# Inverting 32x32 triangles on one Trainium2 core: by columns on VectorE, or as 16x16 blocks with small matmuls for the block below

## The chip, the core and the metric

The kernel runs on one core of a Trainium2 chip. A core has TensorE (PE, matrix products into PSUM), VectorE (DVE), ScalarE (ACT), GpSimd (POOL) and a queue engine (SP) that starts transfers. Each works through its own list of instructions in order; semaphores hold an instruction until what it needs is there. The metric is the device time of one execution in microseconds. All data are float32.

## The reference

The reference has two stages. The first is a linear recurrence over 768 time steps for 4 batches and 8 heads, with a 40x40 state for each of these 32 pairs:

```
y[:, :, t] = np.einsum('bhd,bhde->bhe', rt, state)
Sa = np.einsum('bhde,bhe->bhd', state, at)
state_decay = state * wt[:, :, None, :] - np.einsum('bhd,bhe->bhde', Sa, bt)
state = state_decay + np.einsum('bhd,bhe->bhde', vt, kt)
```

The second takes the outputs as 3072 rows of 320 values. Rows with a positive skip score go to the best of 8 experts (a two-layer network with a ReLU, 320 to 1024 to 320); its result, times a gate, is added to the row. Other rows pass unchanged.

## The kernel before

**Chunks.** The recurrence is worked in 24 chunks of 32 time steps (`for c in range(NC)` in `attn`, lines 469 to 576). Inside a chunk the steps depend on each other through a strictly triangular 32x32 matrix for each of the 32 (batch, head) pairs. Its unit-triangular inverse turns the chunk into matrix products. Four chunks make a phase (`ph, j = divmod(c, 4)`). One "h" is the material of two chunks, so a phase uses two of them, and the 128 triangles of a phase (32 pairs, four chunks) are inverted together, one triangle to a partition.

**What a chunk does**, for each half `x` of the heads (16 pairs): `rs` multiplies the queries with the state; `ux` (line 299) forms the right-hand sides, 128x288 values in PSUM that ACT copies to `UXs`; `uq` (line 310) multiplies them with the inverses in `TB`, and four ACT copies (line 317) put the result into `R1`; POOL masks it (line 319); `sst` (line 320) forms the next state, `yy` (line 342) the output. The next chunk's `rs` needs this chunk's `sst`. The two halves are interleaved by hand. In `uq`, a matrix of `TB` is 128x128, with four 32x32 inverses on its diagonal and zeros elsewhere, and four matmuls of 128 rows, 128 columns and a moving width of 72 do one half.

**Making the inverses.** `m1` (line 154) forms the triangles by small matmuls, for the phase after, and ACT puts them into `AB`. `tinv(ph)` (line 210) inverts them on DVE:

- line 213 transposes `AB` in 32x32 blocks, so that a partition holds one triangle;
- lines 216 and 217 mask, 218 and 219 set the diagonal; columns 0 to 7 of the inverse lie in PSUM (`X0`, tile `px`), columns 8 to 31 in SBUF (`Xi`, in the pool `M`);
- lines 221 to 231 are the solve: 30 steps, each an outer product of a column of the triangle with a row of the inverse (line 228) and a subtraction (line 230), the two groups of columns interleaved;
- line 232 lets ACT copy `X0` beside the rest, and four transposes of 32 partitions by 1024 elements (line 237) put the inverses on the diagonal blocks of `TB`.

`tinv` is a generator. The chunk loop calls `T()` 11 times per chunk (between the pieces above), and each call emits one step; in chunks 1 and 3 every second call emits two. For phases after the first it starts with the last two calls of a phase's first chunk (line 556; in chunk 1 at line 505), and what is left at the end of the phase's fourth chunk is emitted there (line 576). Five phases have one: it works during chunks 1 to 3, 4 to 7, 8 to 11, 12 to 15 and 16 to 19. In the last phase there is none.

**The first phase** is inverted in setup by `tinv0` (line 239), which already uses blocks: the two 16x16 triangles on the diagonal of a 32x32 one are solved together (line 254 the product, 256 the subtraction, 14 steps), and the block below them comes from two sets of small matmuls (`s1`, line 269; `s2`, line 279). `full` (line 271) copies the diagonal blocks to `TB` in four copies of 32 partitions.

**Order.** The order on PE, ACT and DVE is the order of the program (`manual_schedule`); POOL's too in setup. The scans (lines 114 and 126, 1040 elements along a partition) stand in the chunks with even number. DVE also multiplies `rs`'s result by the decay in those chunks (line 296), which `ux` waits for.

Of the kernel before, what the change touches and what calls it, by code (L numbers as in the profile page):

```python
# [57 lines left out]
def attn(ctx,tc,i,m,out,X):  # L58
# [3 lines left out]
    cp=P("const",1); wk=P("wk",1); wk2=P("wk2",2); wk3=P("wk3",3); wk4=P("wk4",4)  # L62
# [91 lines left out]
    def m1(h,x,c,ev=None,late=None,FE=None):  # L154
        if h>=NH: return
        n=h%NL; KB=H[h]['KB']
        if h%2==0 and x==0 and c==0: AB[0]=sq(AB_) if h else sq(a_)
        ab=AB[0]
        p=ps_p.tile([128,4,2,32],F32)
        for hh in range(4):  # L160
            for bb in range(4):
                u=bb*4+hh
                TE.matmul(p[32*bb:32*bb+32,hh],L1[x][n][:,u,c,:],KB[:,u,c],start=True,stop=True)
        o=x*16+(h%2)*8+c
        A.copy(ab[:,:,o:o+7:2].rearrange("p s u -> p u s"),p[:,:,1,:])
        if c==0: an[0]+=1
        if c==0: AT[0]=AT_[an[0]%2].rearrange("p (h c t) -> p h c t",h=4,c=2) if h!=1 else TBa[2][:,8+2*x:10+2*x].rearrange("p h (a t) -> p (h a t)",t=32).rearrange("p (h c t) -> p h c t",h=4,c=2)
        at=AT[0]
        def fin():
            (FE or G).tensor_tensor(at.rearrange("p h c s -> p (h c) s"),at.rearrange("p h c s -> p (h c) s"),mQ.unsqueeze(1).broadcast_to([128,8,32]),ALU.mult)  # L170
            for bb in range(4):
                SP.dma_start(L1[x][n][ao[x]:ao[x]+32,bb*4:bb*4+4].rearrange("p u c t -> p (u c t)"),at[32*bb:32*bb+32].rearrange("p h c s -> p (h c s)"))
        def evac():
            V.transpose(at[:,:,c],p[:,:,0,:])
            if c==1 and late is not None: late.append(fin)
            elif c==1: fin()
        if ev is None: evac()
        else: ev.append(evac)
# [31 lines left out]
    def tinv(ph):  # L210
        ab=AB[0]
        NLt=sq(NL_)
        V.transpose(NLt.rearrange("p a b -> p (a b)"),ab.rearrange("p a b -> p (a b)"))
        Xi=sq(X_)
        X0=ps_x.tile([128,32,SPL],F32)
        V.tensor_tensor(X0,NLt[:,0:SPL].rearrange("p s t -> p t s"),m.mT[:,:,0:SPL],ALU.mult)
        V.tensor_tensor(Xi[:,:,SPL:32],NLt[:,SPL:32].rearrange("p s t -> p t s"),m.mT[:,:,SPL:32],ALU.mult)
        V.memset(X0.rearrange("p a b -> p (a b)")[:,0:SPL*SPL:SPL+1],-1.0)
        V.memset(Xi.rearrange("p a b -> p (a b)")[:,33*SPL::33],-1.0)
        yield  # L220
        for i in range(1,31):
            q=[]
            for g,(j,lo,hi,X) in enumerate(((i,0,min(i,SPL),X0),(i+SPL,SPL,i+SPL,Xi))):
                if j>30: continue
                n=31-j; k=hi-lo
                tmp=tmp_[g]
                tv=tmp[:,:n*k].rearrange("p (a b) -> p a b",b=k)
                V.tensor_tensor(tv,NLt[:,j,j+1:32].unsqueeze(2).broadcast_to([128,n,k]),X[:,j,lo:hi].unsqueeze(1).broadcast_to([128,n,k]),ALU.mult)  # L228
                q.append((tv,X[:,j+1:32,lo:hi]))
            for tv,xv in q: V.tensor_tensor(xv,xv,tv,ALU.subtract)  # L230
            yield
        A.copy(Xi[:,:,0:SPL],X0)  # L232
        s0=(2*ph)%NTB; s1=(2*ph+1)%NTB
        for b in range(4):
            q=slice(32*b,32*b+32)
            t0=TBa[s0]; d=bass.AP(t0.tensor,t0[q].offset,(tuple(t0[q].ap[0]),(TBa[s1].offset-t0.offset,2),(128,16),(1,128)))
            V.transpose(d.rearrange("p h (x f) m -> p m x h f",x=2)[:,q],Xi[q])  # L237
            yield
    def tinv0(Xi):
# [9 lines left out]
        for j in range(1,15):  # L249
# [7 lines left out]
            yield  # L257
        DB=TBa[2][:,12:16].rearrange("p h m -> p (h m)").rearrange("p (a b) -> p a b",a=16)
        V.transpose(fa(NLt[:,16:32]),fa(Xi[:,16:32]))
# [4 lines left out]
        def s1(w,c):  # L264
# [5 lines left out]
            Z[w,c]=wk2.tile([128,8,16],F32,tag="Z",name="Z"); A.copy(Z[w,c],p)  # L270
        def full(w,E):
            for b in range(4):
                q=slice(32*b,32*b+32)
                (V.tensor_copy,A.copy)[E[b]](TBa[w][q,:,q].rearrange("p (x f) m -> p x f m",x=2),NLt[q].rearrange("p m (x h f) -> p h x f m",x=2,h=2)[:,w])
# [35 lines left out]
    def uq(c,x):  # L310
# [3 lines left out]
        for hh in range(4):  # L314
            TE.matmul(UQ[:,hh,:],Tb[:,x*8+hh*2+c%2,:],UXd[x][:,hh,:],start=True,stop=True)  # L315
        for b in range(4):
# [45 lines left out]
    if 1:  # L362

        with tc.manual_schedule(engines={ET.Pool}):
# [104 lines left out]
        for c in range(NC):  # L469
# [144 lines left out]
class Moe:  # L614
    def __init__(s,ctx,tc,i,out,cp):
# [293 lines left out]
```

## Time and profile before

| | us |
|---|---|
| median of 3 runs (689.51 to 695.32) | 689.55 |
| the profiled execution | 686.84 |
| its span | 685.0 |
| setup, to chunk 1's `ux` | 82.9 |
| chunks 1 to 23 and the rows' last routing, to about | 520 |
| the experts, from there to the end | 165 |

The span is the time from the first to the last instruction that the profiler shows. In rows of groups, an entry reads: line, engine, operation, what is written `<-` what is read, the shapes, `x` the count, then the busy time in us and the mean time of one in ns, then the idle time of the engine just before them and what ended it. A matmul in float32 appears as two records, each with a weight load (PEld). [...]

### The profile page before, as it was taken

How to read it: one execution, taken by the hardware profiler on the slowest of the kernel's cores; microseconds unless marked ns; L12 is line 12 of the kernel's file. 1: busy time of each engine (PE TensorE's matmuls, PEld its weight loads, DVE VectorE, ACT ScalarE, POOL GpSimd, SP SyncE). 2: the span in 40 equal slices, each digit the busy share in tenths (PEclk: the TensorE clock that was granted, in tenths of full speed). 3: DMA queues.
4: the chain of work that ended last, by engine and by line, in shares of the span. 5: the costliest groups of instructions: out<-in, count | busy, mean ns of one | idle time of the engine just before them, and what ended most of it. 6: DMA issues, size and time to landing. Idle time of an engine off the chain costs nothing.

```text
span 685.0 us, 31223 instructions
## 1 busy us (share of the span) xinstructions
PE 553.0 (81%) x13620; PEld 473.5 (69%) x13620; DVE 516.1 (75%) x1201; ACT 422.7 (62%) x1154; POOL 324.2 (47%) x248
## 2 busy tenths in 40 slices
PE   5678586778776789866898678997978799999995
PEld 2445475667665668655787567776767689999995
DVE  7999678876997779977699774785339366889881
ACT  6545564576864758747687475877686454444540
POOL 5483942736546365463554533131322236666661
PEclk9788878578996777969779687798897999999998
DMA  7672755352443514435244242435256347677210
GB/s 185 185 239 98 194 138 180 109 161 58 125 132 102 163 50 121 141 102 166 60 129 131 73 126 71 104 110 185 73 158 170 108 127 221 215 214 226 87 49 23
DMA packets 67437, 90.91 MB, mean 133 GB/s; under 512 B 32564, under 2 KB 54657, under 8 KB 65806
## 3 DMA queue, kind: packets, MB, share of 16 engines
q1 hardware_dynamic: 62350, 74.05, 37.2%
q0 software_dynamic: 4944, 14.80, 6.8%
q8 instruction: 109, 1.79, 1.1%
q14 instruction: 34, 0.28, 0.1%
HBM read 74.03 MB, written 17.08 MB: 133 GB/s over the span
## 4 chain that ended last, share of the span: by engine, by line
PE 37%; DVE 29%; ACT 11%; issue 10%; DMA 4%; POOL 3%; POOLq 0%; DVEq 0%; ACTq 0%
DVE M L228 5%; PE pc L786 4%; PE pc L315 4%; PE ps L797 4%; DVE M L126 4%; DVE TB L237 4%; ACT R1t L317 3%; PE ps L327 3%; PE pc L306 3%; PE px L786 2%; PE pc L292 2%; DVE M L230 2%; PE py L797 2%; PE ps L332 2%; ACT L2t L188 2%
## 5 line engine op out<-in xcount | busy, mean ns | idle before, releaser
L319 POOL TENSOR_TENSOR R1t<-R1t,mc 64x512 f32<-64x512 f32 x46 | 62.2, 1353 | 152.2 <-ACT R1t L317 123.7
L317 ACT COPY R1t<-pc 32x288 f32<-32x288 f32 x192 | 74.8, 389 | 30.6 <-PE pc L315 27.5
L315 PE MATMUL pc<-UXs,TB 128*128 128x72 f32 x384 | 66.4, 328 | 0.1
L143 POOL TENSOR_TENSOR WR<-WR,M 128x1024 f32<-128x1024 f32 (+1 forms) x19 | 52.0, 2748 | 23.0 <-DVE M L114 16.9
L734 POOL TENSOR_TENSOR WL<-WR,WH 128x1280 fp32r<-128x1280 f32 (+1 forms) x21 | 57.6, 2779 | 8.7 <-ACT WH L733 8.6
L327 PE MATMUL ps<-R1t,L2t 128*40 128x40 f32 x1472 | 52.4, 228 | 10.9 <-ACT R1t L317 5.1
L315 PEld LDWEIGHTS pc<-UXs,TB 128*128 128x128 f32 x384 | 58.8, 234 | 3.4 <-issue 1.0
L188 ACT COPY L2t<-pq 64x160 f32<-64x160 f32 x184 | 52.6, 286 | 7.0 <-PE pq L185 4.7
L327 PEld LDWEIGHTS ps<-R1t,L2t 128*40 128x40 f32 x1472 | 42.7, 139 | 20.3 <-ACT R1t L317 11.7
L209 ACT COPY R1t<-pq 32x128 f32<-32x128 f32 x184 | 47.0, 256 | 6.5 <-issue 3.0
L228 DVE TENSOR_TENSOR M<-M 128x22 f32<-128x22 f32 (+10 forms) x110 | 49.7, 452 | 0.0
L237 DVE STREAM_TRANSPOSE TB<-M 32x1024 f32<-32x1024 f32 x20 | 38.4, 1919 | 13.7 <-ACT M L232 13.5
L292 PE MATMUL pc<-rvt,SS 128*40 128x32 f32 x1472 | 44.9, 218 | 3.7 <-issue 3.6
L340 ACT COPY SS<-ps 40x320 f32<-40x320 f32 x92 | 38.6, 419 | 14.5 <-PE ps L332 13.0
L688 POOL DMA_INDIRECT xg<-XS,ix x24 | 25.0, 1040 | 46.5 <-DMA xg<-XS,ix 20.9
L292 PEld LDWEIGHTS pc<-rvt,SS 128*40 128x40 f32 x1472 | 38.6, 137 | 11.7 <-issue 8.7
L332 PE MATMUL ps<-L2t,R1t 128*40 128x40 f32 x1472 | 42.7, 220 | 0.4 <-issue 0.4
L308 ACT COPY UXs<-pc 128x288 f32<-128x288 f32 x48 | 19.2, 400 | 36.1 <-PE pc L306 32.1
L230 DVE TENSOR_TENSOR px<-px,M 128x168 f32<-128x168 f32 (+8 forms) x150 | 39.1, 261 | 1.4
L733 ACT CAST WH<-WR 128x1024 fp32r<-128x1024 f32 (+1 forms) x35 | 39.6, 1132 | 0.0
L332 PEld LDWEIGHTS ps<-L2t,R1t 128*40 128x40 f32 x1472 | 38.8, 136 | 0.5 <-issue 0.5
L228 DVE TENSOR_TENSOR M<-M,px 128x168 f32<-128x168 f32 (+8 forms) x150 | 37.0, 247 | 1.7
(244 smaller groups left out, 1577.5 us busy)
## 6 DMA issues: line engine op xcount, KB each, us to landing
rvt<-rv POOLq DMA_DIRECT2D x21, 512.0 KB, 4.6
WR<-kb SPq DMA_DIRECT2D x10, 1024.0 KB
WR<-w SPq DMA_DIRECT2D x16, 640.0 KB
WR<-w SPq DMA_DIRECT2D x16, 512.0 KB
M<-wt SPq DMA_DIRECT2D x9, 520.5 KB
M<-at SPq DMA_DIRECT2D x8, 512.0 KB
WR<-w SPq DMA_DIRECT2D x16, 256.0 KB
R1t<-vt SPq DMA_DIRECT2D x48, 80.0 KB
```

Of the source, the lines that this page charges most:

```text
L143: E.tensor_tensor(H[h]['KB'][0:NR(h),:,:,q,:],H[h]['KB'][0:NR(h),:,:,q,:],v4(Wi)[0:NR(h)],ALU.mult)
L188: A.copy(L2[x][h%NL2][64-64*x:128-64*x,c,bb*4:bb*4+4,:],pt[64*c:64*c+64,:,64*x:64*x+40])
L228: V.tensor_tensor(tv,NLt[:,j,j+1:32].unsqueeze(2).broadcast_to([128,n,k]),X[:,j,lo:hi].unsqueeze(1).broadcast_to([128,n,k]),ALU.mult)
L230: for tv,xv in q: V.tensor_tensor(xv,xv,tv,ALU.subtract)
L237: V.transpose(d.rearrange("p h (x f) m -> p m x h f",x=2)[:,q],Xi[q])
L292: TE.matmul(RS[s,v,:],SS[x][:,b//2,v,:],rr[:,b%2,2*hh+x,:],start=True,stop=True)
L315: TE.matmul(UQ[:,hh,:],Tb[:,x*8+hh*2+c%2,:],UXd[x][:,hh,:],start=True,stop=True)
L317: A.copy(R[uu,4*b:4*b+4,:],UQ[32*b:32*b+32,:,:])
L319: (V if c==NC-1 else G).tensor_tensor(R[pq,:,40:72],R[pq,:,40:72],mQ[pq].unsqueeze(1).broadcast_to([64,16,32]),ALU.mult)
L327: TE.matmul(ST[s,v,:],l2[:,cc,u,:],R[:,u,0:40],start=True,stop=True)
L332: TE.matmul(S2[s,v,:],R[:,u,0:40],l2[:,cc,u,:],start=True,stop=True)
L734: def low(s,E,o,x,h): E.tensor_tensor(s.R(o),x,h,ALU.subtract)
```

## The change

`tinv` is rewritten, `uq` uses 32-row matmuls, and what surrounds them follows.

- `TB` keeps the 32x32 inverses alone: 16 matrices of 128x32 (four inverses above each other, one for each group of 32 partitions) in place of 128x128. So nothing has to be zeroed, and three memsets of `TB` go. `SCR` takes what setup had kept in `TB`'s space.
- The solve handles both 16x16 triangles on the diagonal at once, in a PSUM tile, in 14 steps of two operations.
- Two DVE transposes of 512 elements bring the two solved triangles back to the layout of matmul operands. For the block below the diagonal (the lower solved triangle, times the block of `AB`, times the upper one), two sets of 128 matmuls follow, each of 32 rows, 32 columns and a width of 16, with ACT's copy of the product `Z` between them. `LH` and `LD` are stationary operands, masked by a column of ones and zeros (`m.hi`, `m.lo`), whose other half is filled once by POOL in setup.
- DVE writes the upper rows of `TB` by two multiplications of 256 elements, ACT the lower ones by two copies of 256.
- `uq` does 16 matmuls of 32 rows and 32 columns in place of 4 of 128 by 128, with the same width of 72.
- In setup, `full` is one DVE copy on 128 partitions.

The generator now has 27 steps (35 before). The diff, cut to its core:

```diff
-    TB=cp.tile([128,NTB*2048],F32,name="TB")
-    TBa=[TB[:,2048*q:2048*q+2048].rearrange("p (h m) -> p h m",h=16) for q in range(NTB)]
+    TB=cp.tile([128,NTB*512],F32,name="TB"); SCR=cp.tile([128,2048],F32,name="SCR")
+    LHD=cp.tile([128,2048],F32,name="LHD"); LH,LD=(LHD[:,1024*q:1024*q+1024].rearrange("p (m o) -> p m o",m=32) for q in range(2))
+    TBa=[TB[:,512*q:512*q+512].rearrange("p (h m) -> p h m",h=16) for q in range(NTB)]
...
     def tinv(ph):
-        ab=AB[0]
-        NLt=sq(NL_)
-        V.transpose(NLt.rearrange("p a b -> p (a b)"),ab.rearrange("p a b -> p (a b)"))
-        Xi=sq(X_)
-        X0=ps_x.tile([128,32,SPL],F32)
-        V.tensor_tensor(X0,NLt[:,0:SPL].rearrange("p s t -> p t s"),m.mT[:,:,0:SPL],ALU.mult)
-        V.tensor_tensor(Xi[:,:,SPL:32],NLt[:,SPL:32].rearrange("p s t -> p t s"),m.mT[:,:,SPL:32],ALU.mult)
...
-        for i in range(1,31):
-            q=[]
-            for g,(j,lo,hi,X) in enumerate(((i,0,min(i,SPL),X0),(i+SPL,SPL,i+SPL,Xi))):
...
-                V.tensor_tensor(tv,NLt[:,j,j+1:32].unsqueeze(2).broadcast_to([128,n,k]),X[:,j,lo:hi].unsqueeze(1).broadcast_to([128,n,k]),ALU.mult)
-                q.append((tv,X[:,j+1:32,lo:hi]))
-            for tv,xv in q: V.tensor_tensor(xv,xv,tv,ALU.subtract)
+        ab=AB[0]; fa=lambda t:t.rearrange("p a b -> p (a b)"); TT=V.tensor_tensor
+        NLt=sq(NL_); V.transpose(fa(NLt),fa(ab))
+        V.tensor_scalar(LH[:,0:16],ab[:,0:16],m.hi,None,ALU.mult)
+        yield
+        X=ps_x.tile([128,16,2,16],F32); XB=X.rearrange("p t k s -> p k t s"); xf=X.rearrange("p t k s -> p (t k s)")
...
+        TT(XB,NB.rearrange("p k s t -> p k t s"),m.mT[:,0:16,0:16].unsqueeze(1).broadcast_to([128,2,16,16]),ALU.mult)
+        for k in range(2): V.memset(xf[:,16*k::33],-1.0)
+        yield
+        for j in range(1,15):
+            n=15-j
+            tv=tmp_[j%2][:,:2*n*j].rearrange("p (k a b) -> p k a b",k=2,b=j); xv=XB[:,:,j+1:16,0:j]
+            TT(tv,NB[:,:,j,j+1:16].unsqueeze(3).broadcast_to([128,2,n,j]),XB[:,:,j,0:j].unsqueeze(2).broadcast_to([128,2,n,j]),ALU.mult)
+            TT(xv,xv,tv,ALU.subtract)
             yield
-        A.copy(Xi[:,:,0:SPL],X0)
...
-            V.transpose(d.rearrange("p h (x f) m -> p m x h f",x=2)[:,q],Xi[q])
-            yield
+        NX,DT=(t[:,0:512].rearrange("p (a o) -> p a o",a=16) for t in (X_,NL_)); Z=X_[:,512:1024].rearrange("p (o n) -> p o n",o=32)
+        V.transpose(fa(NX),xf)
+        V.transpose(fa(DT),X.rearrange("p t k s -> p s k t"))
+        V.tensor_scalar(LD[:,0:16],DT,m.lo,None,ALU.mult)
+        yield
+        def prod(L,r):
+            p=ps_x.tile([128,32,16],F32)
+            for q in range(4):
+                for o in range(8*q,8*q+8):
+                    for b in range(4):
+                        u=slice(32*b,32*b+32); TE.matmul(p[u,o],L[u,:,o],r[u,:,o],start=True,stop=True)
+                yield
+            Q.append(p)
+        Q=[]; yield from prod(LH,NX)
+        A.copy(Z,Q[0])
+        yield
+        yield from prod(LD,Z.rearrange("p o n -> p n o"))
+        for w in range(2):
+            t=TBa[(2*ph+w)%NTB].rearrange("p (x f) m -> p m x f",x=2)
+            V.tensor_scalar(t[:,0:16],NX.rearrange("p m (x h f) -> p h m x f",x=2,h=2)[:,w],m.lo,None,ALU.mult)
+            A.copy(t[:,16:32].rearrange("p m x f -> p x f m"),Q[1].rearrange("p (x h f) m -> p h x f m",x=2,h=2)[:,w])
+        yield
...
     def uq(c,x):
...
-            TE.matmul(UQ[:,hh,:],Tb[:,x*8+hh*2+c%2,:],UXd[x][:,hh,:],start=True,stop=True)
+            for b in range(4):
+                q=slice(32*b,32*b+32)
+                TE.matmul(UQ[q,hh,:],Tb[q,x*8+hh*2+c%2,:],UXd[x][q,hh,:],start=True,stop=True)
...
-            zero(fT(0))
...
-            G.memset(fT(1),0.0); G.memset(z[:,512:640],0.0); G.memset(L1t[:,2048:3072],0.0)
+            G.memset(z[:,512:640],0.0); G.memset(L1t[:,2048:3072],0.0)
+            for t in (LH,LD): G.tensor_copy(t[:,16:32],m.mc[:,568:584].unsqueeze(2).broadcast_to([128,16,32]))
...
-            full(0,(0,1,0,1))
+            full(0)
...
-            if c==2: s2(1,1,(0,0,1,1)); G.memset(TBa[2],0.0)
+            if c==2: s2(1,1,(0,0,1,1))
```

More of the change, by code (lines that the diff above doesn't have):

```diff
@@ L166, in m1 @@
         if c==0: an[0]+=1
-        if c==0: AT[0]=AT_[an[0]%2].rearrange("p (h c t) -> p h c t",h=4,c=2) if h!=1 else TBa[2][:,8+2*x:10+2*x].rearrange("p h (a t) -> p (h a t)",t=32).rearrange("p (h c t) -> p h c t",h=4,c=2)
+        if c==0: AT[0]=AT_[an[0]%2].rearrange("p (h c t) -> p h c t",h=4,c=2) if h!=1 else SCR[:,1024+256*x:1280+256*x].rearrange("p (h c t) -> p h c t",h=4,c=2)
         at=AT[0]
@@ L210, in tinv @@
     def tinv(ph):
-        ab=AB[0]
-        NLt=sq(NL_)
-        V.transpose(NLt.rearrange("p a b -> p (a b)"),ab.rearrange("p a b -> p (a b)"))
-        Xi=sq(X_)
-        X0=ps_x.tile([128,32,SPL],F32)
[L216 to L219, printed above, removed]
@@ L220, in tinv @@
-        yield
-        for i in range(1,31):
-            q=[]
-            for g,(j,lo,hi,X) in enumerate(((i,0,min(i,SPL),X0),(i+SPL,SPL,i+SPL,Xi))):
[L224 to L228, printed above, removed]
-                q.append((tv,X[:,j+1:32,lo:hi]))
-            for tv,xv in q: V.tensor_tensor(xv,xv,tv,ALU.subtract)
-            yield
@@ L232, in tinv @@
[L232 to L237, printed above, removed]
-            yield
+        ab=AB[0]; fa=lambda t:t.rearrange("p a b -> p (a b)"); TT=V.tensor_tensor
+        NLt=sq(NL_); V.transpose(fa(NLt),fa(ab))
+        V.tensor_scalar(LH[:,0:16],ab[:,0:16],m.hi,None,ALU.mult)
@@ new lines, in tinv @@
+        yield
+        X=ps_x.tile([128,16,2,16],F32); XB=X.rearrange("p t k s -> p k t s"); xf=X.rearrange("p t k s -> p (t k s)")
+        NB=bass.AP(NLt.tensor,NLt[:,0].offset,(tuple(NLt[:,0].ap[0]),(528,2),(32,16),(1,16)))
+        TT(XB,NB.rearrange("p k s t -> p k t s"),m.mT[:,0:16,0:16].unsqueeze(1).broadcast_to([128,2,16,16]),ALU.mult)
[6 more added lines that the diff above has]
+            TT(xv,xv,tv,ALU.subtract)
+            yield
@@ L257, in tinv0 @@
             yield
-        DB=TBa[2][:,12:16].rearrange("p h m -> p (h m)").rearrange("p (a b) -> p a b",a=16)
+        DB=SCR[:,1536:2048].rearrange("p (a b) -> p a b",a=16)
         V.transpose(fa(NLt[:,16:32]),fa(Xi[:,16:32]))
@@ L270, in s1, with full @@
             Z[w,c]=wk2.tile([128,8,16],F32,tag="Z",name="Z"); A.copy(Z[w,c],p)
[L271 to L274, printed above, removed]
+        def full(w):
+            V.tensor_copy(TBa[w].rearrange("p (x f) m -> p x f m",x=2),NLt.rearrange("p m (x h f) -> p h x f m",x=2,h=2)[:,w])
         def s2(w,c,E):
@@ L281, in s2 @@
                 r=slice(32*b,32*b+16)
-                (V.tensor_copy,A.copy)[E[b]](TBa[w].rearrange("p (x f c) m -> p c x f m",x=2,c=2)[r,c,:,:,32*b+16:32*b+32],p[r].rearrange("p (x f) m -> p x f m",x=2))
+                (V.tensor_copy,A.copy)[E[b]](TBa[w].rearrange("p (x f c) m -> p c x f m",x=2,c=2)[r,c,:,:,16:32],p[r].rearrange("p (x f) m -> p x f m",x=2))
         yield s1,s2,full
@@ L369, in attn @@
             Xi=sq(X_)
-            a1=TBa[2][:,0:8,:].rearrange("p h m -> p (h m)").rearrange("p (u t) -> p u t",u=16)
-            fT=lambda q:TBa[q].rearrange("p h m -> p (h m)")
+            a1=SCR[:,0:1024].rearrange("p (u t) -> p u t",u=16)
             fR=lambda x,n:R1[x][n].rearrange("p u n -> p (u n)")
@@ L482, in attn @@
             uq(c-1,1); T()
-            if c==1: full(1,(0,0,0,0)); m1(3,0,0); m1(3,0,1)
+            if c==1: full(1); m1(3,0,0); m1(3,0,1)
             if c==1: warm(BX[25])
@@ L597, in moe_const @@
     k=np.arange(128)
-    c=np.zeros((128,552),np.float32)
+    c=np.zeros((128,586),np.float32)
+    p=k%32; c[:,552:584]=(np.arange(32)[None]==p[:,None])&(p[:,None]>15); c[:,584]=p>15; c[:,585]=p<16
     c[:,0:32]=np.arange(32)[None]<k[:,None]%32
@@ L620, in __init__ @@
         s.X=dr.tile([3072,DM],F32,name="X")
-        s.mc=cp.tile([128,552],F32,name="mc")
+        s.mc=cp.tile([128,586],F32,name="mc"); s.hi,s.lo=s.mc[:,584:585],s.mc[:,585:586]
         s.wg=cp.tile([128,3,9],F32,name="wg")
```

## The prediction

> **What bounds the kernel now.** I read the page first (busy time and the chain that ended last), then busy time by stretch, then VectorE's (DVE's) groups inside one phase of four chunks.
>
> ```profile
> span 685.0 us, 31223 instructions
> PE 553.0 (81%) x13620; PEld 473.5 (69%) x13620; DVE 516.1 (75%) x1201; ACT 422.7 (62%) x1154; POOL 324.2 (47%) x248
> ...
> PE 37%; DVE 29%; ACT 11%; issue 10%; DMA 4%; POOL 3%; POOLq 0%; DVEq 0%; ACTq 0%
> ```
>
> Neither PE nor DVE bounds the whole: the chain changes between them. So I cut the span at the first `ux` matmul of a chunk. First by groups of chunks (1 to 3, 4 to 7, 8 to 11, 12 to 15, 16 to 19), then chunks 8, 9, 10, 11, 18 and 20 alone. The columns are the stretch, its length, busy PE, weight loads, DVE, ACT, POOL, and the granted clock.
>
> ```profile
> 82.90:156.62 73.72, 55.52 (x1687) 48.26 (x1674) 57.79 (x163) 43.81 (x134) 33.60 (x27) 0.73 0.51 150
> 156.62:243.07 86.45, 66.08 (x2046) 56.34 (x2045) 70.38 (x187) 57.92 (x175) 43.24 (x36) 0.80 0.40 115
> 243.07:327.86 84.79, 66.68 (x2046) 56.73 (x2045) 69.94 (x187) 57.75 (x175) 43.29 (x36) 0.80 0.40 118
> 327.86:412.73 84.87, 67.90 (x2045) 58.15 (x2045) 69.94 (x187) 57.65 (x175) 43.59 (x36) 0.78 0.36 104
> 412.73:482.77 70.04, 59.67 (x1885) 51.55 (x1885) 47.65 (x172) 53.43 (x162) 16.32 (x17) 0.84 0.40 115
> ...
> 243.07:262.95 19.88, 17.74 (x556) 15.54 (x556) 15.53 (x32) 14.00 (x42) 13.04 (x12) 0.76 0.32 92
> 262.95:280.80 17.85, 16.13 (x475) 13.94 (x468) 17.17 (x61) 14.74 (x46) 7.03 (x6) 0.80 0.56 170
> 280.80:305.86 25.06, 16.82 (x552) 14.24 (x551) 22.16 (x64) 13.14 (x41) 13.39 (x14) 0.77 0.33 87
> 305.86:327.86 22.00, 16.00 (x479) 13.02 (x472) 15.09 (x32) 15.87 (x49) 9.82 (x7) 0.89 0.43 133
> ...
> 448.41:461.40 12.99, 11.85 (x457) 10.27 (x456) 12.14 (x56) 10.73 (x34) 5.34 (x5) 1.00 0.32 84
> ...
> 482.77:498.33 15.56, 12.93 (x461) 11.34 (x460) 3.21 (x6) 11.66 (x34) 5.58 (x6) 0.92 0.33 97
> ```
>
> Within a phase the chunks differ. Chunks 8 and 9 leave PE idle about 2 us each; chunk 10 leaves it idle 8.2 us (25.06 less 16.82) with DVE 88% busy, and chunk 11 idle 6.0 us. Chunk 10 holds the last part of the triangular solve together with two scans; chunk 11 ends with the solve's four transposes. This is where DVE sets the end. DVE's groups in one phase (205.84 to 291.79):
>
> ```profile
> L126 DVE TENSOR_TENSOR_SCAN M<-M 128x1040 f32<-128x1040 f32 x3 | 11.2, 3750 | 0.0
> L228 DVE TENSOR_TENSOR M<-M 128x76 f32<-128x76 f32 (+10 forms) x22 | 11.1, 504 | 0.0
> L230 DVE TENSOR_TENSOR px<-px,M 128x168 f32<-128x168 f32 (+28 forms) x30 | 7.8, 260 | 0.3
> L237 DVE STREAM_TRANSPOSE TB<-M 32x1024 f32<-32x1024 f32 x4 | 7.7, 1918 | 3.1 <-ACT M L232 3.0
> L230 DVE TENSOR_TENSOR M<-M 128x76 f32<-128x76 f32 (+10 forms) x22 | 7.6, 345 | 0.0
> L228 DVE TENSOR_TENSOR M<-M,px 128x168 f32<-128x168 f32 (+28 forms) x30 | 7.4, 246 | 0.3
> ...
> L217 DVE TENSOR_TENSOR M<-M,mc 128x768 f32<-128x768 f32 x1 | 2.4, 2441 | 0.0
> ...
> L213 DVE STREAM_TRANSPOSE M<-M 128x1024 f32<-128x1024 f32 x1 | 1.2, 1203 | 0.0
> ...
> L216 DVE TENSOR_TENSOR px<-M,mc 128x256 f32<-128x256 f32 x1 | 0.6, 597 | 0.0
> ```
>
> **DVE, per phase.** The old solve costs 11.1 + 7.8 + 7.7 + 7.6 + 7.4 + 2.4 + 1.2 + 0.6 = 45.8 us of about 71. The first transpose (1.2) stays. For the rest, the setup's own solve in 16x16 blocks, and the spread of the old pairs, give rows:
>
> ```profile
> L254 DVE TENSOR_TENSOR M<-M 128x112 f32<-128x112 f32 x2 | 0.6, 276 | 0.1
> L256 DVE TENSOR_TENSOR M<-M 128x28 f32<-128x28 f32 x2 | 0.4, 198 | 0.1
> ...
> L246 DVE TENSOR_TENSOR M<-M,mc 128x512 f32<-128x512 f32 x1 | 3.0, 3015 | 0.0
> ...
> L259 DVE STREAM_TRANSPOSE M<-M 128x512 f32<-128x512 f32 x1 | 0.7, 714 | 0.0
> L260 DVE STREAM_TRANSPOSE TB<-M 128x512 f32<-128x512 f32 x1 | 1.1, 1061 | 0.0
> ...
> L274 DVE COPY TB<-M 32x512 f32<-32x512 f32 x6 | 3.5, 583 | 0.1
> ```
> ```profile
> L228 DVE TENSOR_TENSOR M<-M,px x150: 150/242/343, 90.4 to 468.1; 128x168 f32<-128x168 f32 x10, 128x30 f32<-128x30 f32 x5, 128x58 f32<-128x58 f32 x5, 128x84 f32<-128x84 f32 x5
> L228 DVE TENSOR_TENSOR M<-M x110: 164/270/2203, 90.6 to 457.9; 128x22 f32<-128x22 f32 x10, 128x42 f32<-128x42 f32 x10, 128x60 f32<-128x60 f32 x10, 128x76 f32<-128x76 f32 x10
> ```
>
> - Steps: 14 multiplies and 14 subtractions of 28 to 112 elements, 0.20 to 0.28 us, mean 0.24: 6.8 us. Here X lies in PSUM, and the pairs with a PSUM operand never took over 0.34 us, where those on SBUF alone went up to 2.2 us; so I add nothing for such stalls.
> - The masked start on 512 elements: 1.2 us (two of the 256-element row) to 3.0 us (L246); I take 1.7, nearer the form with a PSUM output.
> - Two transposes of 512 out of PSUM: 0.7 to 1.1 us each; 1.8 together.
> - Two masking multiplies of 512 by a column, and two of 256 into TB: no row. Below, half of the 0.58 us copy for 256 and that copy for 512; above, the 2.4 us start row for each. I take 0.45 and 0.4: 1.7 together (bounds 1.7 and 9.6, and I stand at the low end because a one-input copy is the nearest operation).
>
> Sum: 1.2 + 6.8 + 1.7 + 0.1 (two small memsets) + 1.8 + 1.7 = 13.3 us (12 to 23). DVE loses **32.5 us of work per phase**, and the 3.0 us wait for the copy at L232.
>
> **PE, per phase.** PE's order in time shows how closely such matmuls follow each other; one matmul is two records, and the last record's own length is taken off.
>
> ```profile
> 45.05 0.58 PE L207 MATMUL px<-rvt 40*32 40x32 f32 x32
> ...
> 60.35 1.29 PE L269 MATMUL pq<-M 32*16 32x16 f32 x128
> ...
> 70.17 1.11 PE L315 MATMUL pc<-UXs,TB 128*128 128x72 f32 x8
> ...
> 82.90 0.70 PE L306 MATMUL pc<-R1t,WR 128*32 128x72 f32 x32
> ...
> 91.08 1.98 PE L315 MATMUL pc<-UXs,TB 128*128 128x72 f32 x8
> ...
> 156.62 1.19 PE L306 MATMUL pc<-R1t,L1t 128*32 128x72 f32 x32
> ```
>
> Added: 2 sets of 128 matmuls of 32x32 by 16, so 512 records. L269 (32x16 by 16) shows (1.29 - 0.18) / 127 = 8.7 ns a record, L207 (32 columns by 32) (0.58 - 0.20) / 31 = 12: 4.5 to 6.3 us. Moved: `uq` goes from 8 records of 128x128 by 72 (about 1.0 us where the clock is full, 1.9 where it is halved) to 32 records of 32x32 by 72. The nearest row is L306, the same width on 128 rows: about 0.5 and 0.9 us. So each `uq` saves 0.5 to 1.0 us, eight per phase 4 to 8. PE comes out between -3.5 and +2.3 us; I take 0. But the additions lie in the third chunk and at the start of the fourth, the savings in all four.
>
> [...]
>
> **Order of the steps.** A chunk calls the solve's generator 11 times, and it starts with the last two of a phase's first chunk. The steps then fill the second chunk and three slots of the third; the transposes fall in its slot 4, the first products in 5 to 8, the copy of Z in 9, the second products in 10, 11 and the fourth chunk's 1 and 2, the writes to TB in 3. The old one ended in the fourth chunk's last slots. PE's new wait is for slot 4's transposes. Queued behind it are `uq` and `rs` of the same chunk, for which ACT's and DVE's copies wait; but between slot 4 and 5 PE has `sst`, and DVE has nothing ahead of the transposes except short operations. I cost it at zero; if DVE were as far behind as in chunk 10 today it would be a few us per phase. ACT gets one 512-element copy and two of 256 and loses one of 256:
>
> ```profile
> L787 ACT ACTIVATE hH<-pc 128x512 fp32r<-128x512 f32 x21 | 12.6, 599 | 38.2 <-PE pc L786 38.2
> L232 ACT COPY M<-px 128x256 f32<-128x256 f32 x5 | 1.9, 372 | 0.1
> ```
>
> That is 0.6 + 0.4 = 1.0 us on an engine 68% busy in a phase. POOL loses two memsets of TB (ACT a third) and gains two fills of 512 in setup, ahead of this idle time of 12.8 us, which hides them:
>
> ```profile
> 62.21 2.90 POOL L319 TENSOR_TENSOR R1t<-R1t,mc 64x512 f32<-64x512 f32 x1 [12.75 <-issue]
> ```
>
> **The sum, by chunks like those that DVE no longer holds.** Chunk 10 does what chunk 8 does (scans, `m1`) plus the products: 19.9 + 1.5 for PE's additions less `uq`'s gain, less 0.9 for fewer steps ahead of the scans: 20.5, so -4.5. Chunk 11 matches chunk 9: 17.85, no longer DVE-bound (DVE was 96% busy there) plus half a product set: 18.0, so -4.0. Chunk 9 itself: DVE falls by about 6 us, PE's 16.1 is next: 16.8, so -1.1. Chunk 8: `uq` alone, -0.6. Together **-10.2 us** per phase in chunks 8 to 11 and 12 to 15. Chunks 4 to 7 are 1.7 longer and get there too: -12. Chunks 1 to 3 hold three of the four with the worst two: -9, and -3 for the TB copies of setup in full width and the lighter second chunk: -12. Chunks 16 to 19 have no scans, so only the transposes' 7.7 + 3.1 us in the last count, less PE's products in a chunk of 13 us: -3. Chunks 20 to 23: `uq`, -1.5. Setup: -1. Sum: -12 - 12 - 20.4 - 3 - 1.5 - 1 = -49.9. The profiled execution took 686.8 us around its span of 685.0; that gives 637, and the median of the runs shown, 689.55, is 2.7 above it: **639 us**. Own range, from the open costs (DVE 8 us per phase up, PE's 3 either way, half of them on the path): 622 to 655.
>
> **Rivals.**
> 1. *The clock recovers as well (about 608 us).* The granted clock is 0.73 to 0.80 in the heavy phases and 1.00 in chunk 18, where PE is 91% busy. If PE's gaps in chunks 10 and 11 go, fewer stretches run at half clock, and chunks 1 to 15 (329.8 us) could come to 16.9 each, a little over chunk 20's 15.6: -76; with 5.5 for setup and chunks 16 to 23, 608. Against it: the scans still leave a gap in two chunks of four. [...]
> 2. *Something else is next (about 664 us).* ACT is 83% busy in chunk 18, and the loop of one chunk (`rs`, `ux`, `uq`, copies, `sst`) runs through it; the scans of 4 us sit ahead of `rs`'s products. Then chunk 10 falls by 2 and chunk 11 by 2.5, some 5 to 6 per phase: -25. For it: chunk 20, with DVE nearly empty, still takes 15.6.
> 3. *The row groups take turns (slower, about 745 us).* If four 32-row groups did not overlap, 512 records would take about 35 ns each, 17.9 us in place of 4.5, and `uq` 1.9 us at full clock in place of 0.5, 11 more per phase: PE gets some 25 us more and becomes the bound at about 91 us per phase, over today's 85, or 97 with the idle tenth that chunk 8 shows: +12 in five phases, -5 for setup and tail. It decides from about 14 ns more per record (10.2 us over 768 records). Against it stands L269's 8.7 ns.
>
> **How the numbers follow.** The forecast 0.62, rival 1 0.13, rival 2 0.19, rival 3 0.06 (half of that a mild form that lands within 1%). A measurement of this kernel can tell about 1% from no change. Faster 0.94, same 0.03, slower 0.03. The range takes half of rivals 1 and 2: 610 to 664.
>
> **What would show it.** DVE busy near 352 us (516 less five times 32.5 and the copies); the groups on TB at 1.9 us gone; 1536 `uq` records at 0.5 to 0.9 us per 32; 2560 product records at 9 to 13 ns; PE idle in chunks 10 and 14 near 4 us in place of 8; no PE wait on the transposes. I am wrong if PE's idle time moves to ACT's copies, if the products' records stand 20 ns or more apart, or if the even chunks stay at 25 us because the scans alone set them.

## The result, and the profile after

The change makes the kernel **slower**: 726.1 us (median of 4) against 691.1 us, a ratio of 1.052 (95% interval 1.045 to 1.059). The forecast was 639 us (610 to 664), on the other side. The page of the changed kernel, whose line numbers are some 10 higher from `tinv` on:

```profile
span 730.8 us, 38275 instructions
PE 582.5 (80%) x17332; PEld 494.1 (68%) x17332; DVE 405.3 (55%) x822; ACT 424.4 (58%) x1161; POOL 324.9 (44%) x248
...
q8 instruction: 138, 2.26, 1.3%
```

DVE lost over 100 us of busy time and PE gained only 30, yet the span of the profiled executions grew by 46 us (the medians by 35). The last line is a transfer queue that the prediction did not look at: it brings instructions, 138 packets of 16 KB. On the page of before its line is:

```profile
q8 instruction: 109, 1.79, 1.1%
```

Where the time went shows by stretch of the changed kernel, cut at `ux` as in the prediction: chunks 1 to 3, 4 to 7, 8 to 15, 16 to 19, and then chunks 6, 7, 8, 9, 10, 11, 18 and 20 alone (columns as there). The granted clock is TensorE's clock as a share of full speed: in the traces of both kernels it is 0.50 or 1.00 at any one time, and a row shows the mean.

```profile
81.15:164.44 83.29, 62.40 (x2322) 53.62 (x2322) 35.35 (x88) 45.71 (x138) 31.99 (x26) 0.69 0.49 138
164.44:257.57 93.13, 75.05 (x2750) 64.34 (x2749) 48.64 (x112) 58.96 (x178) 44.72 (x36) 0.74 0.37 109
257.57:440.03 182.46, 140.63 (x5497) 120.00 (x5497) 94.58 (x224) 117.80 (x354) 89.86 (x73) 0.80 0.36 104
440.03:521.98 81.95, 65.03 (x2590) 56.17 (x2589) 26.93 (x97) 53.69 (x163) 18.12 (x18) 0.79 0.34 99
204.26:237.78 33.52, 26.69 (x1113) 24.23 (x1112) 12.78 (x18) 15.36 (x46) 12.50 (x12) 0.65 0.21 61
237.78:257.57 19.79, 16.43 (x527) 13.52 (x520) 7.17 (x24) 14.70 (x45) 7.26 (x5) 0.80 0.51 150
257.57:278.28 20.71, 15.68 (x605) 13.11 (x604) 17.64 (x28) 14.10 (x41) 16.00 (x13) 0.84 0.31 85
278.28:294.06 15.78, 12.76 (x524) 10.50 (x516) 9.59 (x38) 14.22 (x46) 7.47 (x6) 1.00 0.57 165
294.06:329.90 35.84, 26.71 (x1113) 23.93 (x1112) 13.60 (x23) 15.28 (x46) 14.02 (x14) 0.63 0.27 76
329.90:346.52 16.62, 13.72 (x527) 11.23 (x520) 7.33 (x24) 14.43 (x45) 7.29 (x5) 0.97 0.52 156
474.11:505.31 31.20, 23.60 (x1016) 20.92 (x1015) 5.82 (x17) 13.21 (x40) 6.65 (x6) 0.61 0.17 47
521.98:537.66 15.68, 11.41 (x509) 9.72 (x508) 2.32 (x5) 12.20 (x36) 5.01 (x5) 1.00 0.36 98
```

Chunk 9 gained 2 us, and chunk 20 stands where it stood. The whole loss is in each phase's third chunk, where the products stand: chunk 10 went from 25.1 to 35.8 us, chunk 18 from 13.0 to 31.2, with PE the only engine over half busy. Chunk 18 holds 1016 matmul records in place of 457. Over chunks 1 to 19, PE's idle time with nothing to wait for ("issue") rose from 20 to 66 us, more than the 41 us that these chunks lost, while its waits for DVE fell from 43 to 8. PE's order in chunk 6 shows how it spends such a chunk:

```profile
212.88 0.39 PE L238 MATMUL px<-M,LHD 32*32 32x16 f32 x10 [1.33 <-issue]
213.21 0.65 PE L164 MATMUL pq<-WR,L1t 128*32 128x64 f32 x32
213.79 0.81 PE L301 MATMUL pc<-rvt,SS 128*40 128x32 f32 x32
214.52 0.98 PE L238 MATMUL px<-M,LHD 32*32 32x16 f32 x53
216.98 0.41 PE L238 MATMUL px<-M,LHD 32*32 32x16 f32 x11 [1.48 <-issue]
217.32 0.76 PE L361 MATMUL py<-L2t,R1t 128*32 128x40 f32 x32
218.01 1.10 PE L238 MATMUL px<-M,LHD 32*32 32x16 f32 x64
219.04 0.96 PE L338 MATMUL ps<-R1t,L2t 128*40 128x40 f32 x21
220.87 0.62 PE L338 MATMUL ps<-R1t,L2t 128*40 128x40 f32 x11 [0.87 <-issue]
```

The idle times stand in the middle of a series of products or of `sst`, where nothing is waited for ("issue"). Between two of them lie 11 + 32 + 64 + 21 = 128 records (10 + 32 + 32 + 53 = 127 in the first, one record missing). A record and its weight load are two instructions; 256 instructions at the queue's 16 KB a packet are 64 bytes each. The counts of the pages agree: 2 x 17332 instructions of PE are 135 such blocks, for 138 packets (before, 106 for 109). So PE stops at boundaries of instruction blocks, at six of the nine in this chunk, for 0.4 to 1.9 us. From 212.88 to 216.98, and from there to 220.87, it takes 4.1 and 3.9 us for one block, of which 1.5 and 0.9 us idle. Over chunks 1 to 23, worked out from the packets' start times, no two of them start closer than 3.3 us in the changed kernel (median 3.9). In the five third chunks PE makes 34 stops of over 0.25 us; at 31 of them it goes on 2.2 to 2.9 us after the start of a packet, and the next packet starts 1.0 to 2.6 us later still. The queue's count for chunk 18 before, and then in the changed kernel:

```profile
q8 instruction: 4, 0.07, 2.0%
```
```profile
q8 instruction: 8, 0.13, 1.9%
```

A chunk's time over its blocks, from the rows above and in the prediction: chunk 18 before 13.0 / (457/128) = 3.6 us; after, chunk 18 3.9, chunk 6 3.9. Before, chunk 18 has one such stop, of 0.6 us, and PE is 91% busy, so the array's own work may set its pace. After, chunk 9 also comes to 3.9 us, but PE has no such stop there; it waits for ACT.

### The profile page after: what moved, and what is told of

Read it like the earlier page. It is cut to its first block, busy times and chain, and to the rows that moved or that the text cites. A ratio compares the mean times of both kernels' runs of the same rounds, so it can differ in the third digit from the quotient of the medians.

```text
span 730.8 us, 38275 instructions
## 1 busy us (share of the span) xinstructions
PE 582.5 (80%) x17332; PEld 494.1 (68%) x17332; DVE 405.3 (55%) x822; ACT 424.4 (58%) x1161; POOL 324.9 (44%) x248
## 5 line engine op out<-in xcount | busy, mean ns | idle before, releaser
L330 POOL TENSOR_TENSOR R1t<-R1t,mc 64x512 f32<-64x512 f32 x46 | 65.9, 1433 | 120.9 <-ACT R1t L328 99.7
L238 PE MATMUL px<-M,LHD 32*32 32x16 f32 x2560 | 47.0, 210 | 20.2 <-issue 15.6
L699 POOL DMA_INDIRECT xg<-XS,ix x24 | 25.1, 1044 | 79.2 <-DMA xg<-XS,ix 28.3
L238 PEld LDWEIGHTS px<-M,LHD 32*32 32x32 f32 x2560 | 42.2, 144 | 23.6 <-issue 16.4
L338 PEld LDWEIGHTS ps<-R1t,L2t 128*40 128x40 f32 x1472 | 43.7, 144 | 19.3 <-issue 8.4
L144 POOL TENSOR_TENSOR WR<-WR,M 128x1024 f32<-128x1024 f32 (+1 forms) x19 | 45.9, 2422 | 22.5 <-DVE M L115 16.6
L175 DVE STREAM_TRANSPOSE M<-pq 128x128 f32<-128x128 f32 x40 | 12.3, 312 | 78.1 <-ACT M L166 63.5
L343 PE MATMUL ps<-L2t,R1t 128*40 128x40 f32 x1472 | 46.7, 228 | 10.2 <-issue 10.2
L343 PEld LDWEIGHTS ps<-L2t,R1t 128*40 128x40 f32 x1472 | 42.0, 143 | 11.1 <-issue 11.1
L326 PE MATMUL pc<-UXs,TB 32*32 32x72 f32 x1536 | 42.6, 254 | 5.5 <-issue 5.4
L348 ACT COPY R1t<-ps 40x320 f32<-40x320 f32 x48 | 20.1, 419 | 37.2 <-PE ps L338 36.5
L804 DVE CAST ti<-xe 128x2 int32<-128x2 f32 x8 | 39.8, 4980 | 0.2
```

The lines of the kernel that those rows point to most:

```text
L144: E.tensor_tensor(H[h]['KB'][0:NR(h),:,:,q,:],H[h]['KB'][0:NR(h),:,:,q,:],v4(Wi)[0:NR(h)],ALU.mult)
L238: u=slice(32*b,32*b+32); TE.matmul(p[u,o],L[u,:,o],r[u,:,o],start=True,stop=True)
L326: TE.matmul(UQ[q,hh,:],Tb[q,x*8+hh*2+c%2,:],UXd[x][q,hh,:],start=True,stop=True)
L330: (V if c==NC-1 else G).tensor_tensor(R[pq,:,40:72],R[pq,:,40:72],mQ[pq].unsqueeze(1).broadcast_to([64,16,32]),ALU.mult)
L338: TE.matmul(ST[s,v,:],l2[:,cc,u,:],R[:,u,0:40],start=True,stop=True)
L343: TE.matmul(S2[s,v,:],R[:,u,0:40],l2[:,cc,u,:],start=True,stop=True)
```

## Experiments

**Theory 1**: PE's instructions come a block of 128 records at a time, one in some 3.5 to 3.9 us; a stretch cannot be shorter than its blocks, so the products cost 20 blocks. **Theory 2**: the products cost their own time in the array, at the clock granted. Each run is compared with the kernel before on the same chip. The changed kernel's ratio to compare with is 1.052.

**uq alone.** The kernel before, with only `uq` in 32-row matmuls on the old `TB`:

```diff
-            TE.matmul(UQ[:,hh,:],Tb[:,x*8+hh*2+c%2,:],UXd[x][:,hh,:],start=True,stop=True)
+            for b in range(4):
+                q=slice(32*b,32*b+32)
+                TE.matmul(UQ[q,hh,:],Tb[q,x*8+hh*2+c%2,q],UXd[x][q,hh,:],start=True,stop=True)
```

> The kernel before with one part of the change: uq as 16 matmuls of 32 rows in place of 4 of 128, on the diagonal blocks of the old TB. Theory 1 (PE is held because its instructions come in blocks of 128 matmul records, about 3.6 us each in the changed kernel's dense stretches, and too few instructions there run long enough to hide it): 1152 records more are 9 blocks, spread over all chunks, where a phase of before needs 16 blocks (58 us) of its 85; so little: 689 to 705 us. Theory 2 (what the new matmuls cost is their own time in the array, at a lower granted clock): uq itself gets shorter by 0.5 to 1.0 us, 48 times, part of it on the path: 665 to 685 us.

680.7 us, ratio 0.984 (0.977 to 0.991): below theory 1's range and inside theory 2's. Theory 1 had left out what `uq`'s shorter time gains. Here `uq` in 32 rows is worth 10 us, and its 9 blocks more don't undo that. This part of the change is a small gain.

**No products.**

```diff
-        Q=[]; yield from prod(LH,NX)
+        Q=[xf,xf]
+        for _ in range(4): yield
...
-        yield from prod(LD,Z.rearrange("p o n -> p n o"))
+        for _ in range(4): yield
```

> The changed kernel without its two sets of product matmuls: ACT copies X in place of the products, as long as before, so the lower left blocks of the inverses of phases 1 to 5 are left out of the computation. DVE's relief and the 32-row uq stay. Theory 1: 2560 records less are 20 blocks of about 3.6 us, 72 us less, unless something else is next: 640 to 670 us. Theory 2: 2560 records at the 14 to 16 ns that stand between them in the changed kernel's trace: 36 to 41 us less, 685 to 692 us. If the relief of DVE was worth nothing at all, it stays over 690 us under either.

651.2 us, ratio 0.944 (0.936 to 0.951), as theory 1 said. The products cost 726.1 - 651.2 = 75 us, 29 ns for each of 2560 records, 3.7 us for each of 20 blocks; theory 2 has 41 at most. The rest of the change is worth 40 us in this kernel, which leaves the lower left blocks out.

The clock has a share in this. The five third chunks took 172 us in the changed kernel and 92 here. Of these 80 us, PE's busy time is 61 and its idle time with nothing to wait for 17. The products' own records are only 37 of the 61 (2560 at 14.4 ns); the other records took longer too, at a granted clock of 0.59 to 0.66 in place of 0.74 to 1.00. So the idle time at the boundaries is the smaller part of what is seen in these chunks, and this run alone does not separate the supply from a lower clock.

**Half as many, twice as wide**, and **as many, twice as wide** (the first has `range(8*q,8*q+8,2)`):

```diff
-                        u=slice(32*b,32*b+32); TE.matmul(p[u,o],L[u,:,o],r[u,:,o],start=True,stop=True)
+                        u=slice(32*b,32*b+32); o2=slice(o//2*2,o//2*2+2); TE.matmul(p[u,o2],L[u,:,o],r.rearrange('p n o -> p o n')[u,o2],start=True,stop=True)
```

> The changed kernel with every second product matmul left out and the others twice as wide (32 columns moved in place of 16): half of the products' blocks are computed with the wrong stationary operand. The array moves the same number of columns with half the instructions. Theory 1: 1280 records less are 10 blocks, about 36 us less: 685 to 700 us. Theory 2: the same array time, so 720 to 730 us.

> The changed kernel with all product matmuls, each twice as wide (32 columns moved in place of 16; neighbours overwrite each other's result). The same number of instructions, twice the columns. Theory 1: the block of 128 records still takes as long, so within 1.5% of the changed kernel: 720 to 737 us. Theory 2: the products' array time doubles, 20 to 40 us more: 746 to 766 us.

688.3 us, ratio 0.999 (0.995 to 1.004), and 726.7 us (1.052 as a ratio of medians): theory 1 both times. The second one's four runs spread from 716 to 731 us, so it has no interval. But records at twice the width still stood 14 ns apart, so these two runs separate count from width, not yet supply from a fixed price per record.

**Four times as wide**, with `o4=slice(o//4*4,o//4*4+4)` in the same line:

> The changed kernel with all product matmuls, each four times as wide (64 columns moved in place of 16; neighbours overwrite each other's result). In the run with twice the width the products' records still stood 14 ns apart, so that run raised the array's time by little. At 64 columns and 32 columns of weights, m1's matmuls stand 14 ns apart at full clock and 25 ns at half. Theory 1: a block of 128 records then takes 1.8 to 3.2 us in the array, still under the 3.5 us between two blocks of instructions, so within 1.5% of the changed kernel: 715 to 737 us. Theory 2: 10 ns more for those of 2560 records that run at half clock, 15 to 25 us more: 741 to 751 us.

727.7 us, ratio 1.051 (1.046 to 1.057). The records of the first set stood 27 ns apart in place of 14, at either clock; those of the second set 15 at full clock and 28 at half. Chunk 6, and a series of each set at full clock:

```profile
205.70:237.26 31.56, 26.58 (x1112) 23.42 (x1112) 12.13 (x18) 15.24 (x46) 12.51 (x12) 0.94 0.24 65
```
```profile
209.71 1.97 PE L238 MATMUL px<-M,LHD 32*32 32x64 f32 x64
231.60 1.15 PE L238 MATMUL px<-M,LHD 32*32 32x64 f32 x64
```

That is some 20 us more for the products in the array, and the time did not move. But PE's busy time in the five third chunks did not grow either (134.0 us in place of 131.5), because the clock rose there (0.78 to 0.97 in place of 0.59 to 0.66); PE's idle time with nothing to wait for fell from 36 to 29 us. So this run alone does not exclude that more array time and a higher clock cancelled. It does show that the loss isn't owed to the lower clock alone: at 0.94 chunk 6 still took 31.6 us, 3.6 us for each of its blocks, against 17.5 without products.

**The same instructions, spread.**

```diff
-            yield
+            if j%3==0 or j==14: yield
...
-                yield
+                for _ in range(1+k): yield
...
-        yield from prod(LD,Z.rearrange("p o n -> p n o"))
+        for _ in range(9): yield
+        yield from prod(LD,Z.rearrange("p o n -> p n o"),1)
```

> The changed kernel with the same instructions at other places: three steps of the solve to a call, so that the first set of products falls in the second chunk of a phase (523 matmul records today), and the second set one slice to every second call, mostly in the fourth (527); today six of the eight slices stand in the third, which has 1113. Theory 1 (instructions come in blocks of 128 matmul records, not oftener than one in about 3.5 us, so what counts is how many a stretch needs): the dense chunk falls from 8.7 blocks to about 6.2, the others have some 8 us per phase in which they wait for other things: 680 to 705 us. Theory 2 (each record of the products costs its 29 ns wherever it stands): 718 to 733 us.

724.8 us, ratio 1.035 (1.024 to 1.046; the kernel before took 698.3 us beside it). Theory 1 missed, because I had given the other chunks 8 us of slack per phase; theory 2, in this form a fixed price per record, is met by the time (by the ratio it comes out some 3 us below). Chunks 1 to 19 of the profiled executions say more:

| | records | us | granted clock | us per 128 records |
|---|---|---|---|---|
| before | 9702 | 399.9 | 0.79 | 5.3 |
| changed | 13154 | 440.8 | 0.77 | 4.3 |
| all products, twice as wide | 13154 | 436.9 | 0.82 | 4.3 |
| all products, four times as wide | 13154 | 437.4 | 0.89 | 4.3 |
| the same, spread | 13153 | 438.5 | 0.78 | 4.3 |
| half the products, twice as wide | 11873 | 394.0 | 0.85 | 4.2 |
| no products | 10593 | 361.8 | 0.89 | 4.4 |

The four kernels with the same number of records take the same time within 1%, with other widths, clocks and places, and the time goes with the number. So more array time and a higher clock would have had to cancel each time. Moving instructions gains little; only fewer help. Why the average stays at 4.3 us, over the 3.6 to 3.9 of dense stretches, is not shown.

**uq back at 128 rows**, on block diagonals, and **the same with the products spread**:

```diff
+            for b in range(4):
+                q=slice(32*b,32*b+32)
+                t=TBa[w][q,:,q].rearrange("p (x f) m -> p m x f",x=2)
...
-            for b in range(4):
-                q=slice(32*b,32*b+32)
-                TE.matmul(UQ[q,hh,:],Tb[q,x*8+hh*2+c%2,:],UXd[x][q,hh,:],start=True,stop=True)
+            TE.matmul(UQ[:,hh,:],Tb[:,x*8+hh*2+c%2,:],UXd[x][:,hh,:],start=True,stop=True)
```

> The changed kernel's solve and products with uq as before: 4 matmuls of 128 rows and 128 columns on block diagonals (two TB tiles in place of three, the second one written at the start of the next phase; the inverses are written by four copies of 32 partitions each in place of one). Theory 1: 1152 records less are 9 blocks of about 3.6 us, 32 us less in the dense stretches, against up to 1 us more of array time per uq and more copies: 700 to 718 us. Theory 2 (the array's time is what the products cost): uq's 0.5 to 1.0 us come back 48 times: 735 to 760 us.

> Both: uq with 128 rows and columns, and the products spread as in the run before last. Theory 1: 20 blocks more than before in five phases, none of it in one place, and DVE's relief: 675 to 692 us. Theory 2: 730 to 760 us.

728.6 us, ratio 1.047 (1.038 to 1.055), and 728.8, 1.045 (1.037 to 1.053). Theory 1 missed both; they also lie below theory 2's ranges. Chunks 6 and 7 of the first, which have 48 records fewer than in the changed kernel, show why:

```profile
204.59:235.85 31.26, 28.52 (x1064) 25.80 (x1063) 13.15 (x20) 14.56 (x44) 12.57 (x12) 0.61 0.24 66
235.85:255.48 19.63, 17.45 (x478) 14.76 (x472) 8.30 (x28) 16.17 (x50) 7.77 (x7) 0.76 0.50 151
```

The dense chunk lost 2.3 us, the light one nothing though it has as many fewer: there PE is 17.5 us busy in place of 16.4, with the longer `uq` (and a clock of 0.76 in place of 0.80). A 128-row `uq` needs fewer records, but more of the array.

**Short and long matmuls where nothing else is dense.** The kernel before, with more work for PE in chunks 20 to 22, which have no solve; the second has one matmul of 128x128 by 512 in place of the loop:

```diff
+            if c in (20,21,22) and dn.get(c,0)<8:
+                dn[c]=dn.get(c,0)+1
+                dp=ps_x.tile([128,8,16],F32)
+                for o in range(8):
+                    for b in range(4):
+                        u=slice(32*b,32*b+32); TE.matmul(dp[u,o],m.mc[u,64:96],m.mc[u,192:208],start=True,stop=True)
```

> The kernel before, with 256 matmuls more in each of chunks 20, 21 and 22 (32 rows, 32 columns, width 16, on constants, into a PSUM bank that nothing else uses there, 32 at each of eight calls): 512 records, 4 blocks of instructions. These chunks have no solve, about 459 records and take 15.6 us each. The computation is unchanged. Theory 1: 971 records are 7.6 blocks of 3.6 to 3.8 us, 27 to 29 us, so 12 to 13 us more for each chunk, 35 to 40 us together: 725 to 733 us against a median before of 691. Theory 2: 512 records at 8.5 to 14 ns, 4.4 to 7.2 us a chunk: 703 to 713 us.

> The same place, but one matmul of 128x128 by 512 at each of the eight calls: 16 records more per chunk in place of 512, about 0.86 us of array time each at full clock, 6.9 us a chunk, as much as the 512 short ones or more. Theory 1: no block of instructions more, and the idle time of PE takes part of it: 0 to 5 us a chunk, 691 to 706 us, far from the run with short ones. Theory 2: as much as the short ones or more: 703 to 713 us.

726.0 us, ratio 1.052 (1.047 to 1.057), and 697.8 us, 1.009 (1.005 to 1.012). The short ones cost 35 us without any change to the solve, five times as much as the long ones. Chunk 20 of the two:

```profile
481.55:509.71 28.16, 22.12 (x972) 19.65 (x971) 2.50 (x6) 12.88 (x38) 5.18 (x5) 0.74 0.22 65
```
```profile
485.30:504.35 19.05, 19.05 (x476) 12.53 (x476) 2.50 (x6) 11.86 (x35) 5.11 (x5) 1.00 0.27 74
```

28.16 / (971/128) = 3.7 us a block, with every other engine under half busy. The 512 short records are 4.5 to 6.9 us of array time (8.7 ns apart at full clock, 13.4 at half), the long ones 6.9 (16 records at 0.43 us, the distance of this shape at full clock in the setup of the kernel before), so the array's own time does not tell the two apart; the number of instructions does. A fixed price per record does not fit either: inside a block the records stand that close, and the idle times stand 128 or 256 records apart. The groups' idle time in the run with short ones stands where theory 1 puts it:

```profile
L463 PE MATMUL px<-mc 32*32 32x16 f32 x1536 | 24.2, 197 | 9.7 <-issue 9.7
```

**Without products, the whole computation.** Compact `TB` and 32-row `uq`, the old solve, one transpose in place of four:

```diff
-        for b in range(4):
-            q=slice(32*b,32*b+32)
-            t0=TBa[s0]; d=bass.AP(t0.tensor,t0[q].offset,(tuple(t0[q].ap[0]),(TBa[s1].offset-t0.offset,2),(128,16),(1,128)))
-            V.transpose(d.rearrange("p h (x f) m -> p m x h f",x=2)[:,q],Xi[q])
-            yield
+        t0=TBa[s0]; d=bass.AP(t0.tensor,t0.offset,(tuple(t0.ap[0]),(TBa[s1].offset-t0.offset,2),(32,16),(1,32)))
+        V.transpose(d.rearrange("p h (x f) m -> p m x h f",x=2),Xi)
+        yield
```

> The compact TB and the 32-row uq of the changed kernel, with the old solve by columns on DVE and no products: one transpose on all 128 partitions puts the inverses into TB in place of four of 32 partitions at 1.9 us each. The whole computation is there. Theory 1: the same number of records as the kernel before with uq alone changed (about 681 us), and 6.5 us less DVE work per phase at the place where PE waited for the end of the solve: 650 to 672 us. Its rival, that DVE's work in the fourth chunk was covered anyway: 677 to 685 us.

672.2 us, ratio 0.961 (0.952 to 0.971), at the upper end of theory 1's range. With columns 0 to 15 in PSUM in place of 0 to 7 on top:

```diff
-...; SPL=8; ...
+...; SPL=16; ...
-tmp_=[mv(192) for _ in range(2)]
+tmp_=[mv(240),mv(192)]
```

> The kernel with the compact TB, the 32-row uq and the old solve (no products), with the columns of the inverse split at 16 in place of 8: columns 0 to 15 fill the one PSUM bank, so the large operations read one operand from PSUM, and the solve has 88 operations in place of 104. Worked from the rows of before: 60 operations on 16 columns, 18.6 us, and 28 small ones, 5.6 us, 24 us per phase in place of 34, and without the stalls of pairs on SBUF alone. Theory 1: with PE's records as they were, the relief of DVE counts, as in the run without products (651 us) but a third of it: 655 to 667 us. Rival, that the supply of PE's instructions already sets the whole time of that kernel: 669 to 675 us.

656.1 us, ratio **0.947** (0.943 to 0.951), the fastest version with all of the computation, 10% below the changed kernel. It keeps what was good in the change and takes DVE's relief without the products.

## Why the prediction was wrong, step by step

- **That DVE sets the end of the third and fourth chunks: right.** Taking its work away without products gave 40 us, with `uq`'s 10 in it; 50 were forecast for the whole.
- **The new solve's price: right** (13.3 us forecast). Its groups over five phases:

```profile
L226 DVE TENSOR_TENSOR px<-px,M 128x28 f32<-128x28 f32 (+6 forms) x70 | 17.4, 249 | 2.4
L225 DVE TENSOR_TENSOR M<-M,px 128x28 f32<-128x28 f32 (+6 forms) x70 | 16.3, 232 | 1.8
...
L219 DVE TENSOR_TENSOR px<-M,mc 128x512 f32<-128x512 f32 x5 | 7.1, 1421 | 0.0
L214 DVE STREAM_TRANSPOSE M<-M 128x1024 f32<-128x1024 f32 x5 | 6.0, 1202 | 0.0
L247 DVE TENSOR_SCALAR TB<-M,mc 128x256 f32<-128x256 f32 x10 | 5.4, 623 | 0.0
L215 DVE TENSOR_SCALAR LHD<-M,mc 128x512 f32<-128x512 f32 x5 | 5.3, 1070 | 0.0
L229 DVE STREAM_TRANSPOSE M<-px 128x512 f32<-128x512 f32 x5 | 3.6, 714 | 0.0
L231 DVE TENSOR_SCALAR LHD<-M,mc 128x512 f32<-128x512 f32 x5 | 3.4, 689 | 0.2
L230 DVE STREAM_TRANSPOSE M<-px 128x512 f32<-128x512 f32 x5 | 3.4, 672 | 0.0
```

  Together 67.9 us, 13.6 a phase.
- **DVE's relief of 32.5 us per phase: too large.** In chunks 4 to 7 DVE's busy time fell from 70.4 to 48.6, by 21.7 us; on the whole page it is 405 us, where 352 was forecast. So the old solve had occupied about 21.7 + 13.6 = 35 us and not 45.8: the old operations were interleaved, and in the phase that the prediction read the next one started before the last had ended in 78 of 104 cases; they add up to 33.9 us, but DVE was busy with them for 27.6. Adding their groups counted the difference twice. The run without products shows that this error alone would have left a gain.
- **"PE comes out between -3.5 and +2.3 us; I take 0": this step failed.** It priced 512 records by the distance between records, 8.7 ns from L269, and put the supply of instructions at nothing. That row is a single series of 128 records, as many as one block, so it crosses one boundary at most, and none shows in it as idle time. It can't show what many blocks in a row cost. In the changed kernel the distance inside a block is 14 ns, but a record costs 29 ns with the boundaries and the lower clock: 15 us per phase in place of 4.5 to 6.3. All 512 records of a phase stand in one stretch: chunk 10 was forecast at 20.5 us and took 35.8, while chunks 8, 9 and 11, forecast at 19.3, 16.8 and 18.0, took 20.7, 15.8 and 16.6.
- **`uq`'s saving: right in the array**, 66.4 us of busy time in all before and 42.6 after, 0.5 us each:

```profile
L326 PE MATMUL pc<-UXs,TB 32*32 32x72 f32 x1536 | 42.6, 254 | 5.5 <-issue 5.4
```

  It buys that with 24 records more per `uq`, 1.5 blocks per phase.
- **No wait for the transposes: right but for one.** Over the whole run PE waited for them once:

```profile
PE px L238 <- DVE M L230: 3.8, 1, 3.8
```

- **Rival 3** had the right side and a right threshold (slower from about 14 ns more per record; 20 were measured) with a wrong mechanism: the 35 ns a record that row groups in turns were to cost did not show, as the records stood 14 ns apart inside a block. **Rival 1** ties the half clock to gaps of PE, and the trace of the kernel before shows them together: in chunks 1 to 23 the clock fell from 1.00 to 0.50 21 times, each after 3 us with PE at most 77% busy, and rose 21 times, each after 3 us with PE 100% busy (though from 281 to 284 us PE was half busy and no fall followed). The clock did rise where the products were left out: chunk 6 without them has 0.94, in the changed kernel 0.65.

```profile
186.25:203.74 17.49, 13.65 (x601) 11.71 (x600) 12.06 (x19) 13.04 (x39) 11.45 (x11) 0.94 0.26 70
```

A warning was at hand: in chunk 18 of the kernel before, the densest, PE was 91% busy and took 3.6 us per 128 records. More than doubling its records could not be free, by the array or by the supply; the forecast had -3 us for chunks 16 to 19, and they took 11.9 us more.

## What to carry to other kernels

Count instructions as well as time: for a stretch full of small matmuls, records over 128, times the smallest time per 128 records that any dense stretch of the same kernel shows (3.6 us in the kernel before, in chunk 18), is an estimate of the least that it takes. Work moved from a busy engine to PE in the form of many tiny matmuls can cost more than it frees, and a distance between records taken from one short series doesn't show it. Relief of DVE without the products (a smaller layout, fewer operations, one operand in PSUM) gave 5% here, with the 1.6% of the 32-row `uq` in it.

## What the runs showed of the hardware

- No two instruction packets of 16 KB started closer together than 3.2 us in the kernel before and 3.3 us in the changed kernel. The changed kernel's dense stretches took 3.9 us for 128 records with their weight loads, and 3.6 in chunk 6 with the products four times as wide. After 31 of 34 stops in the third chunks of the changed kernel PE went on 2.2 to 2.9 us after a packet's start, and the next packet started 1.0 to 2.6 us after that. No run changed the packets, so what sets these distances was not shown.
- The products' records stood 14 ns apart at either clock, while the short matmuls of the same shape on constants that lie side by side stood 8.7 ns apart at full clock and 13.4 at half. Both sets of products read their stationary operand with a stride of 32 elements, the first set its moving operand too; whether the stationary stride is the cause of the 14 ns wasn't tried. At four times the width, the set with the strided moving operand stood 27 ns apart at full clock and the one with a contiguous one 15.
